# Mixer kernel: an earlier load of batch 1, two held loads of batch 2, the conv of batch 1 in two halves, and h of group 8 one piece later

## The chip, the cores and the metric

The kernel runs on one core of one Trainium2 chip. The metric is the device time of one execution in microseconds. The profile that is read is of one execution, taken by the hardware profiler; the times are of separate executions.

## The reference

The input x has 8 batches of 4224 positions and 192 channels, in float32. First a causal convolution with 7 taps runs along the positions. Its weights are a softmax over the taps, one set for each of 8 heads of 24 channels:

```
w     = softmax(weight)                          # (8 heads, 7 taps)
y     = causal conv of x with w, per head        # (8, 4224, 192)
h     = (y^T @ U) @ V                            # rank 32, mixes positions
u     = y + h^T
out   = u + relu(u @ w_ch1) @ w_ch2              # 192 -> 768 -> 192
```

U is 4224 x 32 and V is 32 x 4224, so `y^T U` of a batch needs all positions of that batch before any h of it can be made.

## The kernel before, in words

The positions of a batch are cut into 33 tiles of 128, 264 tiles in all. Eight tiles make a group, 33 groups in all; a group can hold tiles of two batches. The whole order of the work is written out by hand[...].

For a batch, the conv is done as matmuls with a banded matrix. Batches 0 and 1 use `conv` (line 351), which makes one head at a time from `x_sb` into two PSUM banks, one for each half of the partitions; each bank is then copied to `y_sb` by `evac` (ACT at line 252 or DVE at line 254, as a letter A or D says). Batches from 2 on use `conv32` (line 317), which reads also a shifted copy `xb_sb` of the batch; GpSimd (POOL) makes that copy in six steps (`x_shift`, lines 289 to 301). `tt_mm` forms y^T U of a batch ("t2" is that of batch 2), `tt_sum` finishes it ("s2"), and `h_group` makes h of one group and adds y on DVE into `u_sb` (line 474), after which SP issues a DMA that transposes `u_sb` into `uT` (line 493).

Then, for a group, `w1` makes relu(u W1) in six chunks of two banks each (matmuls at line 549, relu on ACT at 563 or DVE at 565), and `w2` makes the output of two tiles at a time (line 576), which DVE adds to u into `out_sb` (line 584) and SP stores (line 592). One call of `w2` is called a piece; a group has four.

All of PSUM's tiles come from one pool of eight banks, taken in rotation by `bank()`. The pools of interest beside it: `xs` has 2 buffers for x of a batch, `outs` has 8 for outputs, `us` has 7 and `uts` 5.

`SLOTS` gives the order. Each entry lists the groups whose W1 is done, then the groups whose W2 is done piece by piece, and a table of what is put in front of which piece: "h4" is h of group 4, "d1" the conv of batch 1, "c2:0:3:AAD" three heads of conv of batch 2 from head 0, "x2:4" the first four shift steps of batch 2. A number after the last piece (4 for one group) puts the work behind all pieces.

Loads of x are issued by POOL, a batch in four quarters (`XP`), with a cast to bf16. Those of batch 0 and 1 are issued as POOL comes to them. Those of later batches stand in `LOADS`: a pair (g, m) holds the quarter until the matmuls of chunk m of group g's W1 are done (`held`, a semaphore wait on POOL). The second use of a buffer of `xs` adds a small memset (`x_zero`, line 74).

Of the kernel before, what the change touches and what calls it, by code (L numbers as in the profile page):

```python
# [14 lines left out]
def kernel(  # L15
# [10 lines left out]
    nc = tc.nc  # L26
    P = nc.NUM_PARTITIONS
    B, S, D = x.shape
    H, KC = weight.shape
# [26 lines left out]
    def bank():  # L56
        return psp.tile([P, 512], F32, name="ps", tag="ps")
# [12 lines left out]
    def x_tile(b):  # L70
        xt[b] = xs.tile([P, NB1 + 1, D], BF16, name="x_sb")

    def x_zero(b, eng):
        eng.memzero(xt[b][0:HB, 0, :])

    def x_part(b, r, s0, s1):

        blk = NB0 * r + s0 - 1
        return nc.gpsimd.dma_start(  # L79
            out=xt[b][HB * r : HB * r + HB, s0:s1, :],  # L80
            in_=x[b, blk * HB : (blk + s1 - s0) * HB, :].rearrange("(j p) d -> p j d", p=HB),
        )

    XP = [(0, 1, 17), (0, 17, NB0 + 1), (1, 0, 18), (1, 18, NB1 + 1)]
# [165 lines left out]
    def evac(eng, out, in_):  # L250
        if eng == "A":
            nc.scalar.activation(out=out, in_=in_, func=ACT.Copy)  # L252
        else:
            nc.vector.tensor_copy(out=out, in_=in_)  # L254

    def u_layout(up):
        nb = [nfull + (1 if 32 * jj < nlast else 0) for jj in range(4)]
        for a in range(4):
            for jj in range(4):
                nc.tensor.matmul(  # L260
                    out=up[jj][:, 0 : nb[jj] * R],
                    lhsT=Eq[32 * jj : 32 * jj + 32, a, :],
                    rhs=Ur[32 * jj : 32 * jj + 32, 0 : nb[jj], a * R : (a + 1) * R],
                    start=(a == 0),
                    stop=(a == 3),
                    tile_position=(32 * jj, 0),
                )
        for jj in range(4):
            evac(
                "AD"[jj % 2],  # L270
                U_sb[:, 0 : nb[jj], jj, :],
                up[jj][:, 0 : nb[jj] * R].rearrange("p (k r) -> p k r", r=R),
            )
# [77 lines left out]
    def conv(b, h0, nh, rs, engs, k0=0, k1=NT, pp=None):  # L351

        if yt[b] is None:
            yt[b] = ys.tile([P, NT, D], BF16, name="y_sb")
        nk = {r: min(k1, (NB0, NB1)[r] // 2) - k0 for r in rs}
        if pp is None:
            pp = {r: bank() for r in rs}
        w = nh * GS
        for hh in range(nh):
            h = h0 + hh  # L360
            for halo in range(2):
                for r in rs:
                    for c in range(2):
                        st = 1 - halo + c + 2 * k0
                        nc.tensor.matmul(  # L365
                            out=pp[r][HB * c : HB * c + HB, 0 : nk[r] * w].rearrange(
                                "p (k a) -> p k a", a=w
                            )[:, :, hh * GS : hh * GS + GS],
                            lhsT=bands[h // HQ][
                                HB * r : HB * r + HB, h % HQ, HB * halo : HB * halo + HB  # L370
                            ],
                            rhs=xt[b][
                                HB * r : HB * r + HB,
                                st : st + 2 * nk[r] - 1 : 2,
                                h * GS : h * GS + GS,
                            ],
                            start=(halo == 0),
                            stop=(halo == 1),
                            tile_position=(HB * r, HB * c),
                        )  # L380
        for n, r in enumerate(rs):
            j0 = NB0 // 2 * r + k0
            evac(
                engs[n % len(engs)],
                yt[b][:, j0 : j0 + nk[r], h0 * GS : h0 * GS + w],
                pp[r][:, 0 : nk[r] * w].rearrange("p (k a) -> p k a", a=w),
            )
# [95 lines left out]
    def h_group(g):  # L483
        t0, t1 = g * GT, g * GT + GT
        while t0 < t1:
            b = t0 // NT
            te = min(t1, (b + 1) * NT)
            h_tiles(b, t0 - b * NT, te - b * NT)
            t0 = te
# [77 lines left out]

    out_t = out.rearrange("b s d -> (b s) d").rearrange("(t p) d -> p t d", p=P)

    def w2(g, t0, n):  # L570

        hf, i = t0 // 4, t0 % 4
        cps = bank()
        for a in range(n):
            for m in range(MC):
                nc.tensor.matmul(  # L576
                    out=cps[:, a * D : (a + 1) * D],
                    lhsT=rlt[g][:, m, hf, (i + a) * P : (i + a + 1) * P],
                    rhs=W2_sb[:, m, :],
                    start=(m == 0),  # L580
                    stop=(m == MC - 1),
                )
        o = outs.tile([P, 2, D], F32, name="out_sb")
        nc.vector.tensor_tensor(  # L584
            out=o[:, 0:n, :].rearrange("p n (c k) -> p n c k", c=3),
            in0=cps[:, 0 : n * D].rearrange("p (n c k) -> p n c k", n=n, c=3),
            in1=ut[g][:, i : i + n, :, hf, :],
            op=ALU.add,
        )
        t = g * GT + t0  # L590
        eng = nc.scalar if t + n == NTT else nc.sync
        eng.dma_start(out=out_t[:, t : t + n, :], in_=o[:, 0:n, :])

    def held(ins, after):
        tc.add_manual_dep(
            ins.ins,
            after.ins.name,
            mybir.DependencyInfo(mybir.DependencyClass.Sync, mybir.DependencyReason.DATA),
            reason="load held back",
        )  # L600

    SLOTS = [
        ([0], [], {}),
        ([1], [0], {0: ["h0"], 1: ["h3"]}),
        ([2], [1], {0: ["d1", "h1"], 1: ["t1"], 3: ["s1"], 4: ["h4", "x2:4"]}),
        ([3], [2], {1: ["h5"], 3: ["h6"]}),
        (  # L610
            [4, 5],
# [4 lines left out]
                3: ["c2:3:3:AAD"],  # L616
                4: ["c2:6:2:A", "x3:3"],
                6: ["t2"],
                8: ["s2", "h8"],
                10: ["h9"],  # L620
            },
        ),
    ]
# [1 line left out]
    for k in range(5, 14):  # L625
# [13 lines left out]
        elif k < 10:  # L639
            b = k - 2  # L640
# [11 lines left out]
        SLOTS.append((gs, gs, {p: [w for w in what if w] for p, what in at.items()}))  # L652
    assert nh == NG

    LOADS = {2: [(1, 5), (1, 5), (2, 2), (2, 5)], 3: [(4, 1), (4, 4), (5, 1), (5, 4)]}
    for b in range(4, B):
        g = 3 * b - 6
        LOADS[b] = [(g, 0), (g, 3), (g + 1, 0), (g + 1, 3)]

# [21 lines left out]
        conv(0, h, 2, [0, 1], "AA" if h == 0 else "AD", *KP[0][1:])  # L681
    work = [bank() for _ in range(4)]
    u_layout(work)
    o = 0
    for js in late:
        nc.gpsimd.tensor_copy(
# [42 lines left out]
    yT_part(1, parts1)  # L729
    hT_part(1, parts1)  # L730
    band2 = cst.tile([P, H, QB], BF16, name="band2")
    x_tile(1)
    x_zero(1, nc.gpsimd)
    for xp in XP:
        x_part(1, *xp)
    for r in range(4):
        q = slice(QB * r, QB * r + QB)
# [6 lines left out]
    def do(what):  # L744
        if what[0] == "c":
            b, h0, n, engs = what[1:].split(":")
            conv32(int(b), int(h0), int(n), engs)
            return
        if what[0] == "d":
            for h in range(H):  # L750
                conv(int(what[1:]), h, 1, [0, 1], "AD")
            return
        if what[0] == "x":
            b, n = (int(v) for v in what[1:].split(":"))
            steps.extend(x_shift(b))
            for _ in range(n):
                steps.pop(0)()
            return
        n = int(what[1:])
        if what[0] == "h":  # L760
            h_group(n)
            if n > 1:
                transp(n)
        elif what[0] == "t":
            tt_split(n, tt_mm(n, range(NT)))
        else:
            tt_sum(n)

    for gs1, gs2, at in SLOTS:
        for g in gs1:  # L770
            ends = w1(g, RELU0 if g == 1 else RELU)
            for b, blocks in LOADS.items():
                for q, (gb, m) in enumerate(blocks):
                    if gb == g:
                        if q == 0:
                            x_tile(b)
                            x_zero(b, nc.gpsimd)
                        held(x_part(b, *XP[q]), ends[m])
                        if steps:
                            steps.pop(0)()  # L780
            if g == 0:
                do("h2")
        while steps and gs1 != [3]:
            steps.pop(0)()
        npc = 4 * len(gs2)
        for p in range(npc + 1):
            for what in at.get(p, []):
                do(what)
            if p < npc:
                g, k = gs2[p // 4], p % 4  # L790
                if g == NG - 1 and k == 3:
                    w2(g, 6, 1)
                    w2(g, 7, 1)
                else:
                    w2(g, 2 * k, 2)
# [30 lines left out]
```

## Time and profile before

| | us |
|---|---|
| median of 6 runs | 328.82 (327.7 to 329.45) |
| the profiled execution | 327.45 |
| its span on the core | 325.7 |
| TensorE (PE) busy | 318.6, 98% of the span |
| VectorE (DVE) busy | 269.9, 83% |
| ScalarE (ACT) busy | 170.0, 52% |
| GpSimd (POOL) busy | 143.7, 44% |
| TensorE clock granted | 1.00 throughout |

A line of the timeline gives the start, the time that the merged instructions cover, the engine, the line of the kernel, the operation, the tiles written and read, the shape and the count; in brackets stands how long the engine was idle before it and what ended that. SPq and POOLq are the queues of SP and POOL. Times are from the start of the span. Matmuls are pipelined, so that a line of matmuls covers about 0.17 us more than the time to the next line.

In the order of time: W1 of group 0 starts at 20.29, of group 1 at 24.67, W2 of group 0 at 29.10, W1 of group 2 at 33.97, conv of batch 1 at 37.95, W2 of group 1 at 42.03, W1 of group 3 at 47.56, W1 of groups 4 and 5 at 56.77, conv of batch 2 from 67.30, s2 at 76.46, W1 of groups 6 to 8 at 82.26.

### The profile page before, as it was taken

How to read it: one execution, taken by the hardware profiler on the slowest of the kernel's cores; microseconds unless marked ns; L12 is line 12 of the kernel's file. 1: busy time of each engine (PE TensorE's matmuls, PEld its weight loads, DVE VectorE, ACT ScalarE, POOL GpSimd, SP SyncE). 2: the span in 40 equal slices, each digit the busy share in tenths (PEclk: the TensorE clock that was granted, in tenths of full speed). 3: DMA queues.
4: the chain of work that ended last, by engine and by line, in shares of the span. 5: the costliest groups of instructions: out<-in, count | busy, mean ns of one | idle time of the engine just before them, and what ended most of it. 6: DMA issues, size and time to landing. Idle time of an engine off the chain costs nothing.

```text
span 325.7 us, 9592 instructions
## 1 busy us (share of the span) xinstructions
PE 318.6 (98%) x3998; PEld 221.3 (68%) x3998; DVE 269.9 (83%) x552; ACT 170.0 (52%) x343; POOL 143.7 (44%) x112
## 2 busy tenths in 40 slices
PE   8999999999999999999999999999999999999994
PEld 3757576478467647866864784587796497497494
DVE  7769999987887986998798699879888888896853
ACT  1766724860775397088339609824904903903900
POOL 8592239845986694786869497000000000000000
PEclk9999999999999999999999999999999999999999
DMA  9999993999999899699799956139168079059044
GB/s 105 193 158 172 234 215 99 186 180 195 220 201 189 236 168 169 176 148 201 175 234 154 217 158 185 51 110 248 36 188 248 3 164 274 2 143 245 2 145 148
DMA packets 122907, 53.52 MB, mean 164 GB/s; under 512 B 87760, under 2 KB 122832, under 8 KB 122864
## 3 DMA queue, kind: packets, MB, share of 16 engines
q1 hardware_dynamic: 84528, 38.08, 47.9%
q0 software_dynamic: 38192, 14.73, 41.5%
q8 instruction: 31, 0.51, 0.6%
q14 instruction: 12, 0.10, 0.1%
q10 hardware_dynamic: 144, 0.10, 0.1%
HBM read 29.49 MB, written 25.95 MB: 170 GB/s over the span
## 4 chain that ended last, share of the span: by engine, by line
PE 90%; DMA 5%; DVE 4%; issue 0%
PE ps L576 40%; PE ps L549 36%; DMA uT<-u_sb 5%; PE ps L335 3%; PE ps L452 3%; PE ps L155 2%; PE ps L397 2%; PE ps L365 1%; DVE rl_sb L565 1%; DVE u_sb L474 1%; DVE y_sb L254 1%; PE ps L504 1%; PE ps L519 0%; DVE out_sb L584 0%; DVE band L254 0%
## 5 line engine op out<-in xcount | busy, mean ns | idle before, releaser
L563 ACT ACTIVATE rl_sb<-ps 128x512 bf16<-128x512 f32 x233 | 124.3, 603 | 109.1 <-PE ps L549 97.1
L576 PE MATMUL ps<-W_sb,rl_sb 128*128 128x192 bf16 x1584 | 141.7, 246 | 0.1
L576 PEld LDWEIGHTS <-rl_sb 128*128 128x128 bf16 x1584 | 128.0, 98 | 13.5 <-issue 13.0
L549 PE MATMUL ps<-uT,W_sb 64*128 64x512 bf16 x1188 | 131.6, 376 | 0.3 <-DMA uT<-u_sb 0.3
L565 DVE TENSOR_SCALAR rl_sb<-ps 128x512 bf16<-128x512 f32 x163 | 105.6, 688 | 16.5 <-PE ps L549 16.3
L549 PEld LDWEIGHTS <-W_sb 64*128 64x128 bf16 x1188 | 64.0, 94 | 63.6 <-issue 2.9
L584 DVE TENSOR_TENSOR out_sb<-ps,u_sb 128x384 f32<-128x384 f32 (+1 forms) x133 | 70.4, 550 | 25.6 <-PE ps L576 25.0
L301 POOL COPY xb_sb<-x_sb 32x3072 bf16<-32x3072 bf16 (+1 forms) x24 | 67.7, 2826 | 0.7
L474 DVE TENSOR_TENSOR u_sb<-y_sb,ps 128x192 bf16<-128x192 bf16 (+1 forms) x168 | 66.3, 461 | 0.0
L289 POOL COPY xb_sb<-x_sb 128x3072 bf16<-128x3072 bf16 x12 | 32.7, 2744 | 30.2 <-PE ps L335 16.0
L252 ACT ACTIVATE y_sb<-ps 128x408 bf16<-128x408 f32 (+4 forms) x89 | 37.8, 512 | 10.6 <-PE ps L335 7.8
L79 POOL DMA_DIRECT2D x_sb<-in_x_dram x32 | 27.1, 851 | 22.1 <-PE ps L549 15.2
L254 DVE CAST y_sb<-ps 128x408 bf16<-128x408 f32 (+4 forms) x37 | 19.7, 578 | 1.0 <-PE ps L365 0.9
L452 PE MATMUL ps<-tt_sb,V_sb 32*128 32x192 bf16 x264 | 12.8, 246 | 0.6 <-DVE tt_sb L417 0.2
L335 PE MATMUL ps<-xb_sb,band 64*32 64x384 bf16 x192 | 12.1, 332 | 0.0
L335 PE MATMUL ps<-x_sb,band 64*32 64x384 bf16 x192 | 12.1, 333 | 0.0
L452 PEld LDWEIGHTS <-V_sb 32*128 32x128 bf16 x264 | 4.8, 92 | 8.2 <-issue 8.2
L155 PE MATMUL ps<-zz 128*128 128x512 f32 x12 | 7.3, 752 | 1.5 <-DVE zz L145 1.5
L411 ACT ACTIVATE tt_hi<-ps 128x192 bf16<-128x192 f32 x8 | 2.7, 332 | 11.2 <-PE ps L397 11.2
L365 PE MATMUL ps<-x_sb,band 64*64 64x240 bf16 (+3 forms) x192 | 8.2, 276 | 0.2
L365 PEld LDWEIGHTS <-band 64*64 64x64 bf16 x192 | 6.0, 106 | 2.2 <-issue 1.5
L335 PEld LDWEIGHTS <-band 64*32 64x32 bf16 x384 | 4.5, 89 | 4.1 <-issue 3.0
(65 smaller groups left out, 73.3 us busy)
## 6 DMA issues: line engine op xcount, KB each, us to landing
out_dram<-out_sb SPq DMA_DIRECT2D x131, 192.0 KB, 3.0
x_sb<-in_x_dram POOLq DMA_DIRECT2D x14, 384.0 KB, 8.0
x_sb<-in_x_dram POOLq DMA_DIRECT2D x7, 432.0 KB, 8.6
x_sb<-in_x_dram POOLq DMA_DIRECT2D x7, 408.0 KB, 8.1
x_sb<-in_x_dram POOLq DMA_DIRECT2D x1, 504.0 KB, 7.5
uT<-u_sb SPq DMA_TRANSPOSE x31, 4.0
x_sb<-in_x_dram POOLq DMA_DIRECT2D x1, 480.0 KB, 5.8
W_sb<-in_moe_w_ch_dram POOLq DMA_DIRECT2D x2, 192.0 KB, 7.9
```

The lines of the kernel that those rows point to most:

```text
L79: return nc.gpsimd.dma_start(out=xt[b][HB * r : HB * r + HB, s0:s1, :], in_=x[b, blk * HB : (blk + s1 - s0) * HB, :].rearrange("(j p) d -> ...
L252: nc.scalar.activation(out=out, in_=in_, func=ACT.Copy)
L289: nc.gpsimd.tensor_copy(out=xbt[b][:, s0:s1, :], in_=xt[b][:, s0 + 1 : s1 + 1, :])
L301: nc.gpsimd.tensor_copy(out=xbt[b][q, s0:s1, :], in_=xt[b][q, s0:s1, :])
L335: nc.tensor.matmul(out=pp[r][QB * cg : QB * cg + QB, 0 : nk[r] * GS], lhsT=w[hr], rhs=t[hr, st : st + 2 * nk[r] - 1 : 2, hs], start=True, ...
L452: nc.tensor.matmul(out=banks[pr][:, a * D : (a + 1) * D], lhsT=V_sb[32 * q : 32 * q + 32, (j // 8) * 2 + j % 2, :], rhs=ttb[b][32 * q : 32 ...
L474: nc.vector.tensor_tensor(out=u_group(g)[:, i : i + n, :, hf, :], in0=yt[b][:, run[0] : run[0] + n, :].rearrange("p n (c k) -> p n c k", c=3),
L549: last = nc.tensor.matmul(out=pps[m][hf][:], lhsT=W1_sb[HB * hf : HB * hf + HB, c, m * P : (m + 1) * P], rhs=uTt[g][HB * hf : HB * hf + HB ...
L563: nc.scalar.activation(out=rl[:, m, hf, :], in_=pp[hf][:], func=ACT.Relu)
L565: nc.vector.tensor_scalar_max(out=rl[:, m, hf, :], in0=pp[hf][:], scalar1=0.0)
L576: nc.tensor.matmul(out=cps[:, a * D : (a + 1) * D], lhsT=rlt[g][:, m, hf, (i + a) * P : (i + a + 1) * P], rhs=W2_sb[:, m, :], start=(m == ...
L584: nc.vector.tensor_tensor(out=o[:, 0:n, :].rearrange("p n (c k) -> p n c k", c=3), in0=cps[:, 0 : n * D].rearrange("p (n c k) -> p n c k", ...
```

## The change

- The buffer of batch 1, its memset and its first quarter move ahead of the copies that make `U4_sb`, and so ahead of the loads of V and W2 on POOL. The other three quarters stay where they were.
- The first two quarters of batch 2 were held to the last chunk of W1 of group 1. They are now issued at the third piece of W2 of group 0 and held to the matmuls of its second piece (`done_w2[-1]`). The third and fourth quarter are held to chunks 0 and 3 of W1 of group 2 (before: chunks 2 and 5).
- The conv of batch 1 was one block of eight heads behind W1 of group 2, with ACT and DVE taking one bank of each head. Now four heads stand behind W2 of group 0, ahead of W1 of group 2, evacuated as before; the other four stand behind it, and of their eight banks ACT takes six.
- In slot 4, h of group 8 stood directly behind s2, at piece 8; it now stands at piece 9. h of group 9 moves from piece 10 to piece 11.

```diff
+    done_w2 = []
...
-                nc.tensor.matmul(
+                last = nc.tensor.matmul(
...
+        done_w2.append(last)
...
+    def x_load(b, q, after):
+        if q == 0:
+            x_tile(b)
+            x_zero(b, nc.gpsimd)
+        held(x_part(b, *XP[q]), after)
...
-        ([1], [0], {0: ["h0"], 1: ["h3"]}),
-        ([2], [1], {0: ["d1", "h1"], 1: ["t1"], 3: ["s1"], 4: ["h4", "x2:4"]}),
+        ([1], [0], {0: ["h0"], 1: ["h3"], 2: ["l2:0", "l2:1"], 4: ["d1:0:4:ADADADAD"]}),
+        ([2], [1], {0: ["d1:4:4:ADAAADAA", "h1"], 1: ["t1"], 3: ["s1"], 4: ["h4", "x2:4"]}),
...
-                8: ["s2", "h8"],
-                10: ["h9"],
+                8: ["s2"],
+                9: ["h8"],
+                11: ["h9"],
...
-    LOADS = {2: [(1, 5), (1, 5), (2, 2), (2, 5)], 3: [(4, 1), (4, 4), (5, 1), (5, 4)]}
+    LOADS = {2: [None, None, (2, 0), (2, 3)], 3: [(4, 1), (4, 4), (5, 1), (5, 4)]}
...
     u_layout(work)
+    x_tile(1)
+    x_zero(1, nc.gpsimd)
+    x_part(1, *XP[0])
...
-    x_tile(1)
-    x_zero(1, nc.gpsimd)
-    for xp in XP:
+    for xp in XP[1:]:
         x_part(1, *xp)
...
         if what[0] == "d":
-            for h in range(H):
-                conv(int(what[1:]), h, 1, [0, 1], "AD")
+            b, h0, n, engs = what[1:].split(":")
+            for m in range(int(n)):
+                conv(int(b), int(h0) + m, 1, [0, 1], engs[2 * m : 2 * m + 2])
+            return
+        if what[0] == "l":
+            b, q = (int(v) for v in what[1:].split(":"))
+            x_load(b, q, done_w2[-1])
             return
```

More of the change, by code (lines that the diff above doesn't have):

```diff
@@ L772 @@
             for b, blocks in LOADS.items():
[L773 to L778, printed above, removed]
+                for q, at_end in enumerate(blocks):
+                    if at_end is not None and at_end[0] == g:
+                        x_load(b, q, ends[at_end[1]])
                         if steps:
```

## The prediction

> **What bounds the kernel now.** I read the page first (busy time, then the chain that ended last), then the timeline of each engine around the four places that the change touches.
>
> ```profile
> span 325.7 us, 9592 instructions
> PE 318.6 (98%) x3998; PEld 221.3 (68%) x3998; DVE 269.9 (83%) x552; ACT 170.0 (52%) x343; POOL 143.7 (44%) x112
> PE 90%; DMA 5%; DVE 4%; issue 0%
> ```
>
> TensorE is the bound: 90% of the chain. From 82 us on there is nothing to win: W1 of three groups takes 11.76 us each time (3.92 a group), a W2 piece of 12 matmuls about 1.0 us, and matmuls of different kinds follow each other with the same 0.1 us switch everywhere. All that the change can move is TensorE's waiting before 82 us. It sits in two places. The first is around W1 of group 2 and the conv of batch 1 (PE, then DVE and ACT):
>
> ```profile
> 33.97 4.06 PE L549 MATMUL ps<-uT,W_sb 64*128 64x512 bf16 x36 [0.29 <-DMA uT<-u_sb]
> 37.95 3.37 PE L365 MATMUL ps<-x_sb,band 64*64 64x384 bf16 x64
> 41.77 0.32 PE L452 MATMUL ps<-tt_sb,V_sb 32*128 32x192 bf16 x5 [0.23 <-DVE y_sb L254]
> 38.70 4.00 DVE L254 CAST y_sb<-ps 128x408 bf16<-128x408 f32 x8
> 38.55 3.19 ACT L252 ACTIVATE y_sb<-ps 128x384 bf16<-128x384 f32 x8
> ```
>
> W1 waits 0.3 us for its transposed u. The eight conv heads are worth 8 x 0.335 = 2.7 us of matmuls; they and h1 behind them take 37.95 to 42.03 = 4.08 us instead of about 3.05, because DVE evacuates one bank a head at 0.49 us. The second place is s2 and h8, with the outputs around them (PE, DVE, then SP's queue):
>
> ```profile
> 76.54 0.25 PE L423 MATMUL ps<-tt_lo,R 128*128 128x192 bf16 x1
> 76.72 0.58 PE L452 MATMUL ps<-tt_sb,V_sb 32*128 32x192 bf16 x2
> 77.53 0.34 PE L452 MATMUL ps<-tt_sb,V_sb 32*128 32x192 bf16 x6 [0.23 <-DVE tt_sb L417]
> 79.89 0.34 PE L452 MATMUL ps<-tt_sb,V_sb 32*128 32x192 bf16 x8
> 77.13 0.35 DVE L417 CAST tt_sb<-ps 128x192 bf16<-128x192 f32 x1
> 77.40 2.00 DVE L474 TENSOR_TENSOR u_sb<-y_sb,ps 128x192 bf16<-128x192 bf16 x5
> 79.64 1.05 DVE L584 TENSOR_TENSOR out_sb<-ps,u_sb 128x384 f32<-128x384 f32 x2 [0.24 <-DMA out_dram<-out_sb]
> 80.61 1.94 DVE L474 TENSOR_TENSOR u_sb<-y_sb,ps 128x384 bf16<-128x384 bf16 x4
> 83.40 1.28 DVE L565 TENSOR_SCALAR rl_sb<-ps 128x512 bf16<-128x512 f32 x2
> 67.79 3.20 SPq L493 DMA_TRANSPOSE uT<-u_sb  x1
> 71.08 8.51 SPq L592 DMA_DIRECT2D out_dram<-out_sb  x8
> ```
>
> h8 stands right behind s2 and loses 0.73 us (76.72 to 77.81 for 0.28 us of matmuls and a switch). The DVE lines matter more. The output add of piece 8 waits for a DMA. `outs` has 8 buffers; piece 8 takes the one of piece 0, whose store was issued at 71.08 and landed 8.5 us later, at 79.55, behind the transpose of group 7 (67.79, 11.4 us to landing). In this kernel the wait costs 0.24 us, because the five adds of h8 fill DVE from 77.40 to 79.40.
>
> **The Trainium skill.** "PSUM — Partial Sum Buffer", Specifications: 8 banks a partition. The trace agrees that all eight rotate: the stalls of conv heads 5, 6 and 7 end at 39.81, 40.31 and 40.80, each just after DVE ended the evacuation (39.76, 40.25, 40.74) of the bank taken eight allocations earlier. "DMA: Bandwidth & Descriptors", Issuing engines are not separate DMA queues: loads, stores and transposes run on the same 16 engines. The trace agrees: DMA is 1.50 to 1.59 of 1.6 busy from 66 to 78 us, and a transpose that takes 3.2 us alone (issued at 49.88) takes 11.4 beside two x loads. Same page, Anatomy of one DMA: waits are served by the issuing sequencer before dispatch. So a held load blocks what is behind it in POOL's queue.
>
> **The change, part by part.**
>
> *First load of batch 1 sooner.* One memset (0.17) and one issue (0.83) move from 18.77 to 12.13. POOL was idle there for 1.43 us until U_sb came at 13.56, so the copies and the V loads keep their times. The DMA engines were nearly idle from about 19 to 20.3; 384 KB at about 190 GB/s, 2.1 us, now fills that. V lands about 2.1 us later, near 22.6 (was 20.54 for the fourth piece), before h2 at 24.28; W2 near 24.5, before 29.1. The loads on POOL go round eight semaphores (the fourth W1 load waited until 11.50 for Ur, eight loads ahead of it), so the third and fourth quarter wait for the first quarter and for a V load to land and issue near 21.3 and 22.1, 0.8 us later than now; W2 and the second quarter keep the engines busy until then. Batch 1 is complete near 31.2 instead of 32.49 (21.34 + 11.2). The conv moves from 37.95 to about 33.76, and still finds its data. Worth nothing itself; it makes room for the next two.
>
> *Two loads of batch 2 held.* Issued near 31.65 instead of 29.13. Behind them on POOL: their own successors, and the copies that start when the third quarter lands (45.45). The first held quarter landed at 36.49, after the transpose issued at 26.99 (33.92), so it had stood in line anyway. I put the third quarter at 45.5 +- 1. Behind it POOL has 1.29 us of slack (idle before the load at 58.59). Cost 0.
>
> *Conv in two halves.* First half from 33.76: heads 0 to 2 find banks; head 3 needs the bank of W2's last piece, whose add ends at 35.13. The half ends at 35.6, not 35.2. W1 of group 2 starts at 35.65 (its transposed u is there near 32: the 0.3 us wait is gone) and takes 4.0 including the switch: the DVE casts end at 37.09 and its relus never hold a bank too long. Second half 39.63 to 40.96. Here ACT has six of eight evacuations at 0.37 to 0.39, behind its last relu (39.74): head 4 ends 40.73, head 5 41.11 and 41.50, head 6 41.88. h1's fourth bank is head 5's second: 41.55. W2 of group 1 needs head 6's first: 41.93, against 42.03 before. Gain 0.1 us: DVE's two evacuations less are ACT's two more. Bounds: 1.1 (all stalls gone) and -0.2.
>
> *h8 and h9 a piece later.* Removed: h8's 0.73 us stall. Added: nothing, but the order on DVE is now add 8, five adds of h8, adds 9 and 10, four adds of h9, add 11, relus. Add 8 waits for the landing at 79.55, and now h8 is queued behind it, with DVE idle from 77.48. Walk with the rates of the rows (0.465 a large add, 0.26 a small one, ends about 0.09 after the next start):
> - DVE: add 8 at 79.64, ends 80.20; h8 ends 80.45, 80.71, 81.17, 81.64, 82.10; adds 9, 10 end 82.57, 83.03; h9 83.49, 83.96, 84.42, 84.89; add 11 85.36; relus of chunks 0 and 1 of group 6 end 85.96 and 86.57.
> - PE: pieces 9 and 10 end near 80.2. h9's four banks are those of piece 8 and h8's first three: the fourth at 81.2. Piece 11 needs h8's fourth: 81.67. W1 of group 6 starts at 82.76; chunk 2 waits for h9's third bank (+0.38), chunk 3 for piece 11's (+0.28), chunk 4 for relu 0 (none). It ends at 87.33.
> - Before: 82.26 + 3.92 = 86.18. So +1.15 us, where the matmuls alone would have shown -0.73.
>
> The transpose of group 8 is issued near 82.1 instead of 79.69; with its 7.0 us it lands by 89.1, and W1 of group 8 starts at about 91.2. After that TensorE is the bound, so nothing gives the time back.
>
> Sum: -0.1 + 1.15 = +1.05 us. The profiled execution is 327.45 (span 325.7 and 1.75 around it), so 328.5 there. The six runs have a median of 328.82, 1.37 above it; on that scale 329.9.
>
> **Rivals.**
> *The store lands early* (not slower). From the walk, W1 of group 6 ends 7.7 us after add 8 starts; it breaks even with the early gain when that is at 78.6, i.e. the landing at 78.5, 1.05 sooner. If the landing is before 77.9, h8's stall is simply gone: -0.65 and -0.1, 328.1. For it: 8.5 us is long against the page's median of 3.0. Against: by 50 us the DMA engines have run empty, and what follows (loads held to W1 of groups 4 and 5, copies on POOL, transpose of group 7) hangs on the same TensorE steps as before, so the landing moves with them. A gain is capped too: conv of batch 3 starts at 96.10, and POOL's last copy for it (92.88, 3.08 us) ends at 95.96; more than 0.14 needs batch 3 to land sooner as well.
> *Both places pay* (faster): the landing early and the conv free of ACT: -0.65 and up to -1.1, 327.1. Against: six ACT evacuations are 2.25 us against 1.34 of matmuls.
> *Later still* (slower): in the other runs the landing may be later. Before has about 0.8 us of slack for that (relu 0 ends 84.08, needed at 84.87); the changed kernel has none. Up to +1.9, 330.7; a late transpose of group 8 or a third quarter of batch 2 past 46.7 would add to it.
> *The change does nothing:* the two moves cancel, 328.8. That takes a landing near 78.5.
>
> **How the numbers follow.** 0.3% is 0.99 us, about what a measurement of this kernel can tell from no change. Forecast (+0.6 to +1.5) 0.45, of it 0.32 above 0.99; later still 0.20; early landing, with the cancelling case, 0.20; both pay 0.15. Slower 0.52, same 0.33, faster 0.15. The range leaves out about half of "both pay" and the tail of "later": 327.6 to 331.0. The likeliest case alone: 329.4 to 330.3.
>
> **What would show it.** Right: add 8 of slot 4 with an idle of about 2 us ended by an output DMA, h8's adds after it near 80; PE stalls at h9, piece 11 and inside W1 of group 6, whose end is about 1 us later; no stall at h8; W1 of group 2 without a wait; W2 of group 1 about where it was (41.9). Wrong: store 0 landing before 78.5, W2 of group 1 before 41.5, a wait of conv or h2 for a load, or POOL's copies of batch 2 holding its conv (67.3).

## The result, and the profile after

The changed kernel takes 331.42 us (median of 34 runs, 326.5 to 333.71), the kernel before 328.58 in the same comparison (69 runs). The ratio of the compared runs is 1.0037, 95% interval 1.0021 to 1.0054: slower, and clear of the noise. That ratio leaves out the changed kernel's runs over 1.5% above its fastest, about half of them, so it understates: the plain medians differ by 2.84 us, 0.9%.

The page of the changed kernel's profiled execution (331.59 us): span, busy times, the granted clock in 40 slices, and the chain that ended last.

```profile
span 329.8 us, 9592 instructions
PE 321.2 (97%) x3998; PEld 225.3 (68%) x3998; DVE 269.2 (82%) x550; ACT 171.2 (52%) x345; POOL 143.7 (44%) x112
PEclk9999999999997999999999999999999999999999
PE 89%; POOL 5%; DVE 3%; ACT 1%; issue 1%
```

DMA, 5% of the chain before, has gone from it, and POOL, which was not in it at all, holds 5%. In one slice, the thirteenth, TensorE's clock drops. The timeline of the changed kernel says where (POOL, then DVE and PE):

```profile
33.13 1.65 POOL L79 DMA_DIRECT2D x_sb<-in_x_dram  x2 [7.56 <-PE ps L578]
49.04 2.75 POOL L289 COPY xb_sb<-x_sb 128x3072 bf16<-128x3072 bf16 x1 [7.79 <-DMA x_sb<-in_x_dram]
61.76 0.82 POOL L79 DMA_DIRECT2D x_sb<-in_x_dram  x1 [0.33 <-PE ps L549]
96.64 3.08 POOL L301 COPY xb_sb<-x_sb 32x3456 bf16<-32x3456 bf16 x1
79.54 0.56 DVE L587 TENSOR_TENSOR out_sb<-ps,u_sb 128x384 f32<-128x384 f32 x1 [0.33 <-PE ps L578]
79.44 0.42 PE L452 MATMUL ps<-tt_sb,V_sb 32*128 32x192 bf16 x8
83.24 11.90 PE L549 MATMUL ps<-uT,W_sb 64*128 64x512 bf16 x108
97.16 0.33 PE L335 MATMUL ps<-xb_sb,band 64*32 64x384 bf16 x1
99.78 0.50 PE L335 MATMUL ps<-xb_sb,band 64*32 64x408 bf16 x1 [2.29 <-POOL xb_sb L301]
100.93 2.10 PE L578 MATMUL ps<-W_sb,rl_sb 128*128 128x192 bf16 x12
```

The same steps of POOL in the timeline of the kernel before:

```profile
29.13 1.65 POOL L79 DMA_DIRECT2D x_sb<-in_x_dram  x2 [4.37 <-PE ps L452]
45.60 5.43 POOL L289 COPY xb_sb<-x_sb 128x3072 bf16<-128x3072 bf16 x2 [5.86 <-DMA x_sb<-in_x_dram]
58.59 0.82 POOL L79 DMA_DIRECT2D x_sb<-in_x_dram  x1 [1.29 <-PE ps L549]
92.88 3.08 POOL L301 COPY xb_sb<-x_sb 32x3456 bf16<-32x3456 bf16 x1
```

One thing first. The ten matmuls on zeros with which TensorE begins (line 155) took 7.53 us in this execution and 6.20 in that of before. W1 of group 0 starts at 21.43 here and at 20.29 before, and over the twelve profiles that the experiments below left it starts anywhere from 20.11 to 21.43, by chance: four of them have the same instructions up to there, and start it at 20.11, 20.29, 20.36 and 20.81. I count from that start, so 1.14 us come off the times above before they are compared.

Counted so, the two held loads are issued 2.9 us later, the copies that wait for them begin 2.3 us later, and POOL's last copy for the conv of batch 3 ends 2.6 us later. Before, that copy ended 0.14 us ahead of the conv's first matmul (95.96, 96.10). Now the conv issues one matmul, and TensorE then stands idle for 2.29 us by the line. From the start of that matmul to the start of the next it is 2.62 us (97.16 to 99.78); in the kernel before, the first eight start within 0.03 us, so that 2.6 us is what the wait costs. And then TensorE runs slowly: a W2 piece takes 2.10 us instead of 1.16. The windows view gives for each stretch the busy times, and behind them the granted clock, the DMA share and GB/s:

```profile
33.00:35.00 2.00, 2.00 (x30) 1.80 (x32) 2.00 (x6) 0.00 (x0) 1.65 (x2) 1.00 0.37 104
99.70:103.00 3.30, 3.22 (x43) 2.03 (x46) 1.05 (x2) 1.68 (x4) 0.83 (x2) 0.50 1.37 233
```

In the 3.3 us after the wait the clock that TensorE is granted is half. The first of these lines is for later: in the 2 us in which the held loads are issued, the DMA engines move only 104 GB/s.

The account of TensorE, from the starts of W1 in the two traces:

| interval | before | changed | difference |
|---|---|---|---|
| W1 of group 1 to W1 of group 3 (conv of batch 1, W2 of groups 0 and 1) | 22.89 | 22.76 | -0.13 |
| W1 of group 4 to W1 of group 6 (conv of batch 2, h8) | 25.48 | 25.46 | -0.02 |
| W1 of group 6 to W1 of group 9 (conv of batch 3) | 28.23 | 32.32 | +4.09 |
| all else, to the last matmul | 224.41 | 224.41 | 0 |
| last matmul to the end of the span | 4.38 | 3.44 | -0.94 |

The sum is +3.0 us, close to the 2.84 between the medians; with the start's 1.14 it makes the 4.1 between the spans. The second row hides two changes: h8's stall is gone (-0.7), and the conv of batch 2 waits for POOL (TensorE idle for 0.6 us before 69.26). The last row was not forecast.

### The profile page after: what moved, and what is told of

The parts are those of the page before. It is cut to its first block, busy times and chain, and to the rows that moved or that the text cites. A ratio compares the mean times of both kernels' runs of the same rounds, so it can differ in the third digit from the quotient of the medians.

```text
span 329.8 us, 9592 instructions
## 1 busy us (share of the span) xinstructions
PE 321.2 (97%) x3998; PEld 225.3 (68%) x3998; DVE 269.2 (82%) x550; ACT 171.2 (52%) x345; POOL 143.7 (44%) x112
## 4 chain that ended last, share of the span: by engine, by line
PE 89%; POOL 5%; DVE 3%; ACT 1%; issue 1%
PE ps L578 39%; PE ps L549 36%; POOL xb_sb L301 4%; PE ps L335 3%; PE ps L452 3%; PE ps L155 3%; PE ps L397 2%; POOL x_sb L79 1%; PE ps L365 1%; ACT rl_sb L563 1%; DVE u_sb L474 1%; DVE out_sb L587 1%; ACT y_sb L252 0%; PE ps L519 0%; PE ps L504 0%
## 5 line engine op out<-in xcount | busy, mean ns | idle before, releaser
L549 PEld LDWEIGHTS <-W_sb 64*128 64x128 bf16 x1188 | 67.3, 94 | 60.7 <-issue 3.8
L252 ACT ACTIVATE y_sb<-ps 128x408 bf16<-128x408 f32 (+4 forms) x91 | 38.7, 509 | 19.2 <-PE ps L335 12.6
L79 POOL DMA_DIRECT2D x_sb<-in_x_dram x32 | 27.1, 850 | 22.6 <-PE ps L549 13.7
L254 DVE CAST y_sb<-ps 128x408 bf16<-128x408 f32 (+4 forms) x35 | 18.9, 579 | 3.9 <-PE ps L335 3.1
L335 PE MATMUL ps<-xb_sb,band 64*32 64x384 bf16 (+1 forms) x192 | 13.2, 343 | 2.9 <-POOL xb_sb L301 2.9
L335 PE MATMUL ps<-x_sb,band 64*32 64x384 bf16 x192 | 12.5, 345 | 0.0
L155 PE MATMUL ps<-zz 128*128 128x512 f32 x12 | 8.6, 875 | 1.5 <-DVE zz L145 1.5
```

Source lines behind the costliest of these rows:

```text
L79: return nc.gpsimd.dma_start(out=xt[b][HB * r : HB * r + HB, s0:s1, :], in_=x[b, blk * HB : (blk + s1 - s0) * HB, :].rearrange("(j p) d -> ...
L335: nc.tensor.matmul(out=pp[r][QB * cg : QB * cg + QB, 0 : nk[r] * GS], lhsT=w[hr], rhs=t[hr, st : st + 2 * nk[r] - 1 : 2, hs], start=True, ...
L549: last = nc.tensor.matmul(out=pps[m][hf][:], lhsT=W1_sb[HB * hf : HB * hf + HB, c, m * P : (m + 1) * P], rhs=uTt[g][HB * hf : HB * hf + HB ...
```

## The experiments

Theory A is that the held loads cost it all: they make POOL late, and the conv of batch 3 waits. Theory B is the forecast's own: h8 stands behind the add that waits for a store. Four kernels take the parts apart.

**Loads of batch 2 put back,** the rest as changed:

```diff
-        ([1], [0], {0: ["h0"], 1: ["h3"], 2: ["l2:0", "l2:1"], 4: ["d1:0:4:ADADADAD"]}),
+        ([1], [0], {0: ["h0"], 1: ["h3"], 4: ["d1:0:4:ADADADAD"]}),
...
-    LOADS = {2: [None, None, (2, 0), (2, 3)], ...
+    LOADS = {2: [(1, 5), (1, 5), (2, 0), (2, 3)], ...
```

> The changed kernel with one part undone: the first two quarters of batch 2 go back to the end of W1 of group 1 (third and fourth stay at chunks 0 and 3). Theory A (the held loads make the copies of batch 2 and 3 on GpSimd late, and the convs of batches 2 and 3 wait): the third quarter lands near 45.5 us again, first copy near 45.7, no wait of 0.3 us or more ahead of either conv. If A is all of the loss, the time is at or below the kernel before by 0.1 to 0.8 us. Theory B (h8 and h9 a piece later put the adds of h8 behind an output store): the first store of slot 4 lands near 79.5, the ninth add waits about 2 us for it, and the kernel is still 0.8 to 1.5 us slower than before.

Measured: 327.07 us, ratio 0.9958 (0.9938 to 0.9978). Timeline, POOL then DVE and PE:

```profile
44.42 5.43 POOL L289 COPY xb_sb<-x_sb 128x3072 bf16<-128x3072 bf16 x2 [4.33 <-DMA x_sb<-in_x_dram]
78.56 0.56 DVE L587 TENSOR_TENSOR out_sb<-ps,u_sb 128x384 f32<-128x384 f32 x1 [1.23 <-DMA out_dram<-out_sb]
81.71 12.46 PE L549 MATMUL ps<-uT,W_sb 64*128 64x512 bf16 x108
```

The copies begin early, no conv waits, the clock stays, and a kernel slower than before has become a faster one. Undoing that one part takes the whole loss away. With it B's wait comes back, smaller than forecast: VectorE idles 1.23 us, not about 2, before the add, and W1 of groups 6 to 8 takes 12.46 us (11.90 in the changed kernel).

**h8 and h9 later, alone,** in the kernel before:

```diff
-                8: ["s2", "h8"],
-                10: ["h9"],
+                8: ["s2"],
+                9: ["h8"],
+                11: ["h9"],
```

> The kernel before with h of group 8 at piece 9 and h of group 9 at piece 11, nothing else. The prediction's walk (theory B): the ninth output add of slot 4 waits about 2 us for the landing of the first, W1 of group 6 ends about 1.1 us later, time +1.15 us. Theory A gives this part 0 to -0.7 us: h8's stall of 0.73 us goes away, and what is won is lost again ahead of the conv of batch 3, which can start no more than 0.14 us sooner.

Measured: 328.72 us, ratio 1.0007 (0.9993 to 1.0021). Timeline, DVE:

```profile
79.61 0.56 DVE L584 TENSOR_TENSOR out_sb<-ps,u_sb 128x384 f32<-128x384 f32 x1 [1.41 <-DMA out_dram<-out_sb]
80.08 2.00 DVE L474 TENSOR_TENSOR u_sb<-y_sb,ps 128x192 bf16<-128x192 bf16 x5
```

B's mechanism is there: the add waits for the store, and the five adds of h8 stand behind it. Its size is smaller. Counted from the start of W1 of group 0 the store landed 0.58 us sooner than before, which leaves 1.15 - 0.58 = +0.57; the end of W1 of group 6 moved by +0.60, of which 0.2 is a longer wait of W1 of group 2. In the times the part can't be told from nothing.

**Early first quarter and the conv in halves, alone,** in the kernel before:

```diff
-        ([1], [0], {0: ["h0"], 1: ["h3"]}),
-        ([2], [1], {0: ["d1", "h1"], ...
+        ([1], [0], {0: ["h0"], 1: ["h3"], 4: ["d1:0:4:ADADADAD"]}),
+        ([2], [1], {0: ["d1:4:4:ADAAADAA", "h1"], ...
```

> The kernel before with the early first quarter of batch 1 and the conv of batch 1 in two halves, nothing else. The prediction's walk: W1 of group 2 without its 0.3 us wait, W2 of group 1 0.1 us sooner, time -0.1 us (between -0.4 and +0.2). If the conv in two halves were a cause of the loss, W2 of group 1 would start over 0.3 us later, counted from the start of W1 of group 0.

Measured: 327.09 us, ratio 0.9955 (0.9938 to 0.9972). The two intervals sum to 22.76 us, 0.13 less than before, as forecast, but the time fell by 1.35. In the trace 0.95 us of that stand behind the last matmul: 3.42 us to the end of the span instead of 4.38.

**Early first quarter and the held loads, alone,** in the kernel before:

```diff
+        ([1], [0], {0: ["h0"], 1: ["h3"], 2: ["l2:0", "l2:1"]}),
...
+    LOADS = {2: [None, None, (2, 2), (2, 5)], ...
```

> The kernel before with the early first quarter of batch 1 and the first two quarters of batch 2 held to the second piece of W2 of group 0 (third and fourth quarter as before), nothing else. Theory A: the first copy of batch 2 starts 1.5 to 3.5 us later than before, the convs of batches 2 and 3 wait together over 1.5 us, time +1.5 to +3 us. The prediction (held loads cost nothing): first copy within 1 us of before, no such wait, time within 0.3 us of before.

Measured: 333.47 us, ratio 1.0153 (1.0128 to 1.0178). Timeline, POOL and PE:

```profile
48.20 2.74 POOL L289 COPY xb_sb<-x_sb 128x3072 bf16<-128x3072 bf16 x1 [8.28 <-DMA x_sb<-in_x_dram]
100.37 0.33 PE L335 MATMUL ps<-xb_sb,band 64*32 64x408 bf16 x1 [3.29 <-POOL xb_sb L301]
```

The windows view of a stretch that begins 2.6 us after that wait:

```profile
103.00:104.50 1.50, 1.50 (x23) 1.02 (x8) 1.05 (x2) 1.50 (x4) 0.00 (x0) 0.50 1.52 179
```

The held loads alone are worth 5 us, more than the 1.5 to 3 expected: W1 of group 6 to that of group 9 takes 33.34 us (+5.11), of which 3.63 is the wait (96.74 to 100.37) and 1.5 is left for the halved clock after it. It ends as before, 4.37 us behind the last matmul. Theory A stands.

What remained was the gain at the end, seen up to here in every kernel with the conv in halves and in no other. Those kernels move two evacuations from VectorE to ScalarE (heads 5 and 7). The end of the span is set by stores, and in the kernels with the long end the DMA view shows an instruction fetch beside them. Does it follow the place of the conv, or the number of VectorE's instructions? Two kernels separate these.

**Halves without the moved evacuations:** the conv in halves alone, with this besides.

```diff
-        ([2], [1], {0: ["d1:4:4:ADAAADAA", "h1"], ...
+        ([2], [1], {0: ["d1:4:4:ADADADAD", "h1"], ...
```

> e3_conv_only with the second half of the conv of batch 1 evacuated in plain alternation (ADADADAD), so that no instruction moves from VectorE to ScalarE; the place of the conv and the early load stay. Theory 1 (the two moved evacuations shift a late instruction fetch, which spares the last three stores about 1 us at the end): from the last matmul to the end of the span it takes about 4.4 us again (3.42 in e3_conv_only), and the time is about 328.0, some 0.9 above e3_conv_only's 327.09. Theory 2 (the shorter end comes with the place of the conv): it stays at 3.4 and the time near 327.1. Both: the two intervals of W1 that hold the halves sum to 22.7 to 22.95 us.

**Moved evacuations without the halves:**

```diff
-                conv(int(what[1:]), h, 1, [0, 1], "AD")
+                conv(int(what[1:]), h, 1, [0, 1], "AA" if h in (5, 7) else "AD")
```

> The kernel before with only the evacuations of two heads of the conv of batch 1 changed (heads 5 and 7: both by ScalarE, as the change has them), the conv left in one piece. Theory 1 (moved evacuations shift the instruction fetch): the end takes about 3.4 us in place of 4.38 and the time is about 327.5, ratio near 0.997. Theory 2 (the end belongs to the place of the conv): 4.4 us at the end, and the time is that of before, 328.5 within 0.3.

Measured: 327.36 us, ratio 0.9977 (0.9963 to 0.9991), end 4.46 us, for the halves alone; 327.40, ratio 0.9969 (0.9953 to 0.9985), end 3.44, for the moved evacuations alone. The DMA view of the last 5 us of stores (a queue with packets, MB and share; then an issue group with KB and the median us to landing), first of the halves:

```profile
q14 instruction: 1, 0.01, 1.0%
out_dram<-out_sb SPq DMA_DIRECT2D x1, 96.0 KB, 3.0
out_dram<-out_sb ACTq DMA_DIRECT2D x1, 96.0 KB, 2.9
```

and of the moved evacuations:

```profile
out_dram<-out_sb SPq DMA_DIRECT2D x1, 96.0 KB, 1.7
out_dram<-out_sb ACTq DMA_DIRECT2D x1, 96.0 KB, 1.7
```

The end goes with the two instructions and not with the conv. With the fetch (one packet of 8 KB) beside them the last stores need 1.2 us more to land. The halves gave 0.29 us in this trace, the better with plain alternation (the second half's interval is 12.07 us, 12.24 with six of eight on ScalarE). Their time was expected near 328.0 and is 0.6 below that. It is 0.8 us under the kernel before, with an interval of 0.3 to 1.2, which does not tell whether that is more than the 0.29.

Nor does the 0.29 us need the halves. In the four profiles without the early first quarter of batch 1 the transpose for W1 of group 2 lands 13.6 to 14.0 us after the start of W1 of group 0, and W1 of group 2 waits 0.29, 0.43, 0.49 and 0.67 us. In the eight with it the transpose lands at 11.9 to 12.5, and nothing waits. One of the eight, the held loads alone, has the conv whole, and its two intervals sum to 22.52 us, against 22.60 and 22.76 with the halves and 22.89 before. So the early load is enough to take the wait away, and with it in place the halves cost 0.1 to 0.2 us.

**The store's wait taken away:** the loads put back, as in the first experiment, and the pool `outs` with 10 buffers instead of 8.

> e1_loads_back with ten output buffers in place of eight: what makes the output add after the second piece of W2 of group 4 wait for a store is taken away, with h8 and h9 left at their later places. Theory of the prediction (h8's adds are held by that wait, and h9, piece 11 and W1 of group 6 by them): that add waits for TensorE alone, W1 of group 6 takes 11.9 us (12.46 in e1_loads_back) with no wait for uT inside, and the time is 0.4 to 0.6 below e1_loads_back's 327.07. Rival (W1 of group 6 is held by VectorE's queue whatever the store does): W1 of group 6 stays near 12.4 us, and the time is 327.1 within 0.3.

Measured: 327.41 us, ratio 0.9973 (0.9960 to 0.9987). Timeline, DVE and PE:

```profile
77.58 0.56 DVE L587 TENSOR_TENSOR out_sb<-ps,u_sb 128x384 f32<-128x384 f32 x1 [0.33 <-PE ps L578]
81.29 11.90 PE L549 MATMUL ps<-uT,W_sb 64*128 64x512 bf16 x108
96.63 0.33 PE L335 MATMUL ps<-xb_sb,band 64*32 64x408 bf16 x1 [1.09 <-POOL xb_sb L301]
```

As theory B has it, the add waits for TensorE alone and W1 of groups 6 to 8 takes 11.90 us. But the time missed what I expected, 0.4 to 0.6 below 327.07. TensorE came to the conv of batch 3 0.9 us sooner than with eight buffers, while the last quarter of batch 3 landed 1.5 us later (why it did is open), so that the conv waited for POOL. And the trace has three more records of VectorE's instructions, 708 in place of 705, with the long end back (4.26); ScalarE's number is the same in both, 386.

**The kernel before once more:**

> The kernel before as it is, profiled once more: how much room its GpSimd copies of batch 3 leave ahead of the conv of batch 3 in another execution. In the first profile the last copy ended 0.14 us ahead of the first matmul that needs it. If that room is chance, this execution shows a wait between 0 and 1 us there, or none with another margin; the end after the last matmul is 4.4 us in both.

Measured: 327.94 us. POOL's last copy ends 0.47 us ahead of the conv of batch 3 (96.08, 96.55), the end is 4.42. So the room there is some tenths in both executions. W1 of group 2 waits 0.67 us here, instead of 0.29.

**The held loads one piece sooner,** the rest as changed:

```diff
-        ([1], [0], {0: ["h0"], 1: ["h3"], 2: ["l2:0", "l2:1"], 4: ...
+        ([1], [0], {0: ["h0"], 1: ["h3", "l2:0", "l2:1"], 4: ...
```

> The changed kernel with the two held loads of batch 2 released one piece sooner, by the first piece of W2 of group 0 (about 1.7 us sooner than the changed kernel, still about 1.1 us later than before). If the stall is the lateness left over when each queue's slack is used up, GpSimd's copies of batch 3 come about 1.7 us sooner than the changed kernel's and the conv of batch 3 waits 0 to 0.9 us for them (2.45 in the changed kernel), with no fall of the granted clock: 327.1 to 328.2 us. If being issued among W2's pieces costs as such (the transfers that they meet there), the wait stays over 2 us and the time over 330.

Measured: 326.99 us, before 327.81 on that chip, ratio 0.9975 (0.9961 to 0.9990). Timeline:

```profile
30.53 1.65 POOL L79 DMA_DIRECT2D x_sb<-in_x_dram  x2 [4.94 <-PE ps L452]
57.92 0.17 POOL L74 MEMSET x_sb<- 64x96 uint32 x1
58.44 0.82 POOL L79 DMA_DIRECT2D x_sb<-in_x_dram  x1 [0.34 <-PE ps L549]
91.89 3.08 POOL L301 COPY xb_sb<-x_sb 32x3456 bf16<-32x3456 bf16 x1
```

The first load of batch 3 in the kernel with the loads of batch 2 put back, where W1 of group 0 starts at the same time, 20.27:

```profile
58.44 0.82 POOL L79 DMA_DIRECT2D x_sb<-in_x_dram  x1 [2.34 <-PE ps L549]
```

The held loads are issued 1.4 us sooner than in the changed kernel (10.26 after the start of W1 of group 0; 11.70), and the wait is gone, with 1.6 us to spare (94.97; the conv at 96.54). The last 1.4 us of the delay decide, not the place among W2's pieces. The lines show why: POOL comes to the first load of batch 3 2.0 us later than with the loads put back (the 2.34 have become 0.34), yet issues it at the same time. All of that delay, and nothing beyond it, fitted into POOL's slack; the changed kernel's did not.

**Ten output buffers and fewer instructions on VectorE:** as with ten buffers, and one evacuation of the conv of each of batches 4 to 7 by ScalarE.

```diff
-                1: [f"c{b}:0:3:AAD"],
+                1: [f"c{b}:0:3:AADAAA"],
```

> e7_ten_outs with one evacuation of the conv of each of batches 4 to 7 moved from VectorE to ScalarE, four instructions fewer on VectorE. In the ten runs so far the late instruction fetch beside the last stores was there with 707 or 708 VectorE records and not there with 705. So here it is gone: the end after the last matmul takes 3.4 us in place of e7_ten_outs's 4.26, and the time is 0.5 to 0.9 below its 327.41, if ScalarE's longer queue in these convs costs less than 0.1 us each. Rival (the fetch doesn't follow VectorE's count): the end stays at 4.3 and the time at 327.4 or above.

Measured: 326.22 us, ratio 0.9946 (0.9929 to 0.9964): 0.5% under the kernel before. It is the lowest ratio here, though its interval overlaps those of the loads put back and of the halves. The end takes 3.35 us with 704 records on VectorE. The four convs cost 0.1 us each: W1 to W1 is 28.14 to 28.37 us in place of 28.05 to 28.28.

## Why the prediction was right, and where it was not

The forecast was 329.9 us and slower. By the ratio, 1.0037 x 328.82 = 330.0, it is met; by the plain median, 331.42, it is 1.5 short and 0.4 above the range. That the sum agrees is luck. The part that was to make the kernel slower cost nothing in it, a part put at nothing cost about 4 us, and a gain that was not forecast took almost 1 us of that back.

*First load of batch 1 sooner, cost 0: right, and it pays.* V was there at 23.06, W2 at 25.24, and batch 1 was complete at 32.19. Less the start's 1.14 that is 21.9, 24.1 and 31.05 (forecast 22.6, 24.5, 31.2), and nothing waited. It was said to be worth nothing itself; as shown above, it is enough to take away the wait of W1 of group 2, 0.3 us in the profile of before that was read and up to 0.7 in others.

*Two loads of batch 2 held, cost 0: the step that failed.* It said "it had stood in line anyway. I put the third quarter at 45.5 +- 1", and set that against 1.29 us of slack on POOL. The third quarter landed at 48.89, 47.75 less the start. The argument took the DMA engines to be busy until the load's turn. They were not: the transpose ahead of it landed at 33.69, and the windows view, shown above, has 104 GB/s from 33 to 35 us. The next 4 us, and the nearest 6 us of the kernel before, counted from W1 of group 0:

```profile
35.00:37.00 2.00, 1.91 (x35) 0.97 (x29) 2.00 (x5) 1.64 (x4) 0.00 (x0) 1.00 1.22 124
37.00:39.00 2.00, 2.00 (x22) 1.09 (x20) 2.00 (x5) 1.44 (x3) 0.85 (x1) 1.00 1.29 126
```

```profile
32.00:34.00 2.00, 1.71 (x23) 1.48 (x22) 2.00 (x5) 0.00 (x0) 0.00 (x0) 1.00 1.17 200
34.00:36.00 2.00, 2.00 (x20) 0.93 (x22) 2.00 (x5) 1.13 (x2) 0.00 (x0) 1.00 1.58 194
36.00:38.00 2.00, 2.00 (x24) 0.75 (x24) 1.53 (x3) 1.95 (x5) 0.85 (x1) 1.00 1.43 219
```

So the engines ran short of work while the loads were held, and moved 104 to 126 GB/s for 6 us instead of about 200. The first packet of the held loads starts 1.7 us after their issue (34.79, 33.13); in the kernel before, the loads of batch 1 still run through that time, to 32.49. Part of the low rate is this lag; why they stayed near 125 once the loads were running is open. (The forecast also took 1.6 as the limit of the DMA share; it is none, from 29 to 31 us the changed kernel has 2.16.) Of the 2.9 us by which the issue is later than before, 2.3 passed on to the third quarter's landing. The experiments say it more sharply. The kernel with the loads put back, the one with them a piece sooner and the changed kernel issue the third quarter at the same time, 16.49 us after the start of W1 of group 0, and it lands at 24.00, 25.98 and 27.46: holding the two loads in front of it for 1.4 and 2.9 us longer makes it 2.0 and 3.5 us later.

With the 0.62 us that POOL waits between its copies for the fourth, POOL is 3.0 us late behind them (its memset at 61.25, before 57.12). The slack took only 0.96 of that: 0.33 of the 1.29 stand between memset and load also here, where W1 of group 4 had begun at 57.79 and TensorE had long released the load, issued at 61.76. So 2.0 us went on to the loads of batch 3. Their third and fourth quarter were now issued behind the transpose of group 7 (from 69.13 on, the transpose at 68.80; before 65.96 and 67.79), and the last landed at 82.19, 81.05 less the start, instead of 78.43. The forecast named this way, "a third quarter of batch 2 past 46.7 would add to it", and the 0.14 us of room at the conv of batch 3, but the first only in a rival and the second only as a cap on a gain. The measured price is +4.1 us in the changed kernel and +5.1 alone.

*Conv in two halves, -0.1: right in size, together with the early load.* It is -0.13 in the changed kernel and -0.13 in the run with the early load and the halves alone. The wait of W1 of group 2 is gone as forecast, but the early load alone would have taken it away. ScalarE bounds the second half, as forecast: it is 0.17 us shorter when VectorE gets its two evacuations back.

*h8 and h9 a piece later, +1.15: right mechanism, wrong size, and in the changed kernel not at work.* Alone it is +0.4 to +0.6 us in the profile. The mis-sized term is the landing, 0.58 us sooner than in the one execution that it was read from; over the ten profiles other than those of the changed kernel and the held loads alone it comes 58.05 to 59.44 us after the start of W1 of group 0 (59.26 in the one read). In the changed kernel store 0 landed at 77.28, 76.14 less the start. There the transpose of group 7 was issued ahead of the two loads instead of behind them; that this is the cause is argued, not tested. It is the forecast's own sign of being wrong ("store 0 landing before 78.5"): the place cost nothing there and paid 0.7.

*Not in the forecast:* -0.94 at the end, where an instruction fetch no longer lies beside the last stores, and about 1.5 of the +4.1, which is left for the clock after the wait.

Of the rivals, "later still" named what came, a third quarter past 46.7. "The store lands early" had the landing right and the sign wrong. "Both places pay" and "the change does nothing" fall.

Left open in part: how far the spread of the changed kernel's runs (326.5 to 333.71) follows the wait at the conv of batch 3. One profile shows a long wait, and the fastest run has room for none, but no profile of that run exists. The mean granted clock that is on record for each run goes further. One stretch of 3.4 us at half lowers the mean of such a run to 0.995. It is 0.995 or less in 20 of the 34 runs, with a median of 331.70 us, and 0.998 or more in the other 14, with a median of 329.90. (In the kernel before it is 0.995 or less in 4 of 108 runs, all at 331.66 us or more.) So the clock falls in some runs and not in others, and the 1.8 us between the two is near the price that the profile shows for it. What spreads the runs within each kind isn't shown.

## What to carry to other kernels

Before putting the delay of a load at nothing because its queue is full, look whether the queue is full *because of that load*: here the transfers ahead had landed, the DMA engines ran short, and the load behind came late by the whole delay and more. Then follow the delay through the slack to the tightest margin down the chain, here 0.14 us, some 60 us later. And where a change moves instructions between engines, look at what lies behind the last matmul, not only at the work.

## What the runs showed of the hardware that was not expected

- *The end is about 1 us longer where an instruction fetch lies beside the last stores.* In all twelve profiles the end after the last matmul is 4.08 to 4.46 us with 707 or 708 records of VectorE's instructions in the trace and 3.35 to 3.44 with 704 or 705. In the first kind a fetch of 8 KB starts 24.5 to 24.9 us after the last block of W1 (groups 30 to 32) starts, just after the last stores are issued; in the second it comes when they have landed. The last three stores land in 2.5 to 3.2 us in the first kind and in 1.7 to 1.9 in the second. That the two moved instructions decide the end is shown; that the fetch itself slows the stores, and how, isn't.
- *A wait of TensorE costs more than its length.* TensorE stood idle for 2.29 us in the changed kernel and for 3.29 with the held loads alone. In both the clock was then granted at half for 3.41 us, and the interval grew by 1.5 us beyond the wait, a little less than half of that. In the first the half rate began as the wait ended, in the second 1.5 us after. After the wait of 1.09 us with ten buffers the clock stayed at 1.00. In the clock record of these traces every whole stretch is a multiple of 3.413 us (27 of them at full rate, one at half and 67 at full in the changed kernel), as if the clock were set by windows of that length. Laid on that grid, the windows after which it fell had TensorE idle for 2.2 and 1.9 us, and windows with 1.4 (the one before the second fall) and 1.1 us (ten buffers) left it alone. The Trainium skill ("TensorE: Matmul & The Clock Gate", Part 1) puts the fall to half rate after an idle window of about 3.4 us; the length agrees with the traces, but here a window idle for little more than half was enough. Two falls do not give a threshold.
- *The cost of a delayed load isn't linear in the delay.* Held 1.4 us longer than before, the loads cost nothing that the times show: POOL's slack took it. Held 2.9 us longer, they cost 4.1 and 5.1 us in the interval that holds the conv of batch 3.
